# Gated attention and Fourier mixing on one core: the order of the projections' sums, fillers and maxima

## The chip, the cores and the metric

The kernel runs on one core of a Trainium2 chip. A core has five engines with queues of their own: TensorE (PE; PEld is its weight load), VectorE (DVE), ScalarE (ACT), GpSimd (POOL) and SyncE (SP), which here issues the DMA transfers. Engines run at once and wait for one another by semaphores; within a queue the order is fixed. The metric is the device time of one execution in microseconds (us). The time before is the median of three runs.

## The reference

Only what is computed; x is [2048, 640] and S = 2048, D = 640, 32 heads of 20.

```python
def reference(A_x, A_wqkv, A_wo, B_x, B_dft_seq_re, B_dft_seq_im, B_dft_hid_re, B_dft_hid_im, gate_w):
    def _A_ref(x, wqkv, wo):
        ...
        q, k, v = qkv[0], qkv[1], qkv[2]
        scores = jnp.einsum("bhqd,bhkd->bhqk", q, k) * (Dh ** -0.5)
        p = _softmax(scores, axis=-1)
        o = jnp.einsum("bhqk,bhkd->bhqd", p, v)
        return (lambda x, *d: x.transpose(*d))(o, 0, 2, 1, 3).reshape(B, S, D) @ wo
    def _B_ref(x, dft_seq_re, dft_seq_im, dft_hid_re, dft_hid_im):
        a = jnp.einsum("bsd,ed->bse", x, dft_hid_re)
        b = jnp.einsum("bsd,ed->bse", x, dft_hid_im)
        y = jnp.einsum("ts,bse->bte", dft_seq_re, a) - jnp.einsum("ts,bse->bte", dft_seq_im, b)
        return y
    x = A_x
    g = _sigmoid((x * gate_w).sum(-1, keepdims=True))
    a = _A_ref(x, A_wqkv, A_wo)
    b = _B_ref(x, B_dft_seq_re, B_dft_seq_im, B_dft_hid_re, B_dft_hid_im)
    return g * a + (1 - g) * b
```

## The kernel before

All products are made from float32 values cut in two parts of fewer bits ("split": ACT or POOL casts the high part, DVE or POOL subtracts to get the low one), three matmuls for one product (`three`, L118 to L120).

The program has a prologue and a long steady part. The prologue, about 276 us, makes q, k and v; the steady part walks 32 units of attention (scores, exponentials, p times v) with the Fourier products between them as filler. The change is in the prologue alone. Its pieces:

- **x** is four blocks of 512 rows, `xs[0]` to `xs[3]`, each loaded as raw float32 into `pair_tile`s (pool "p", seven of them) and split (`load_x`, `load_first`).
- **q and k tiles**: five column tiles c of 128 for q and five for k. Tile 0 is projected plainly for each block (`qk_tiles`, 30 matmuls). Tiles 1 to 4 are projected by **quads** (`quad`): for a **group** g of two blocks, x block 2g and 2g+1, a quad makes q and k of column c in seven products instead of eight, p6, p7, p1, p5, p2, p4, p3 in that order, 54 matmuls with 512 columns. It needs sums of x over its two blocks (s1 to s5, `load_sums`, made on POOL and split by ACT and DVE) and sums of weights (`load_pair`, which gives three steps: `sums` on POOL, L403 to L407; `ready`, the first set of parts, "t"; `parts`, the second set, "b", one of its two casts by POOL in the second group). PE's products go to PSUM banks, of which six rotate; ACT and DVE add them up (L444), POOL adds one output (L459) and cuts the outputs in parts (L115), and SP stores them to `qk_scr`. Between its products a quad calls `between(k)`, where the next quad's steps are hung in.
- **Value pairs** (`v_pair(hf, s)`, 30 matmuls): v of half the heads for two tiles of 128 rows. POOL fills the tile with ones, ACT copies the products into it, SP stores it.
- **Maxima**: the attention needs row maxima of the scores before its exponentials. `run_s` issues steps of two score matmuls each (L196); DVE reduces each bank (L198). 41 steps (82 maxima) are done ahead in the prologue. They read the first **stack** of q and k rows, twelve loads from `qk_scr` (`load_stack`).
- **Segments** (`lead`): eight tiles of the hidden-dimension Fourier product are made in the prologue, fifteen pieces of two matmuls each (L511), with maxima between the pieces; they need `wb` weights 2, loaded by `load_wb(2)`.

The order is written out by hand in the program, line after line: an instruction's place in its engine's queue is where the code issues it. In the order before: blocks 0 and 1, value pairs, quads of the first group, blocks 2 and 3, value pairs with maxima, quads of the second group with two segments each. SP's queue takes every load and store in that order as well, and an issue waits for a free semaphore lane and for what its transfer reads.

## Time and profile before

| | |
|---|---|
| time, three runs | 1861.7, 1864.7, 1865.28 us; median 1864.7 |
| the profiled execution | 1868.31 us, its span 1866.5 us |
| mean granted TensorE clock | 0.993 |
| busy | PE 1841.1 us (99%), DVE 1448.6 (78%), ACT 1392.5 (75%), POOL 1057.8 (57%) |
| HBM | 224.97 MB read, 64.05 MB written |

In the profile a row of a timeline is: start in us, duration, engine, line, operation, out<-in, shapes, count, and in brackets the engine's idle time before it and what ended that. A busy time of a stretch counts overlapping matmuls once, and matmul ends are modelled, so PE can read as busy while it goes slowly; the distance from one matmul's start to the next says more. Releasers are inferred from semaphores. The span lies within the execution's own time.

### The profile page before, as it was taken

To read this page: it belongs to the slowest core of one execution; us is meant where nothing else is said; L and a number is where in the kernel's file an instruction comes from. 1 tells how busy PE (TensorE), PEld (TensorE's weight loads), DVE (VectorE), ACT (ScalarE), POOL (GpSimd) and SP (SyncE) were. 2 spreads that over 40 slices of the span, in tenths; PEclk is the share of its full clock that TensorE was granted. 3 is DMA by queue.
4 is the path that set the end of the run, shared out by engine and by line. 5 is a ranking of instruction groups with operands and counts; after the bars stand their busy time and mean duration, and the time that the engine had idled before them with its cause. 6 is when DMAs were issued, how large, how long until landed. Compare 5 with 4: busy or idle time off the path is not lost.

```text
span 1866.5 us, 44873 instructions
## 1 busy us (share of the span) xinstructions
PE 1841.1 (99%) x17520; PEld 1359.7 (73%) x17520; DVE 1448.6 (78%) x2426; ACT 1392.5 (75%) x2716; POOL 1057.8 (57%) x859
## 2 busy tenths in 40 slices
PE   9998999999999999999999999999999999999998
PEld 8787776776767777777777777777777777776666
DVE  4535777878878888888888888888888888888853
ACT  4543337878878888888888888888878877778885
POOL 4654663212126677344578778655668867745544
PEclk9998999999999999999999999999999999999999
DMA  7576334121226576545567586746586776531333
GB/s 251 180 244 166 111 131 123 46 78 58 75 61 170 177 224 194 149 125 143 179 192 237 166 242 200 199 148 168 175 230 192 209 206 194 178 94 49 88 99 108
DMA packets 185467, 291.95 MB, mean 156 GB/s; under 512 B 48211, under 2 KB 116435, under 8 KB 185255
## 3 DMA queue, kind: packets, MB, share of 16 engines
q1 hardware_dynamic: 185255, 289.09, 51.9%
q8 instruction: 137, 2.24, 0.5%
q14 instruction: 75, 0.61, 0.1%
HBM read 224.97 MB, written 64.05 MB: 155 GB/s over the span
## 4 chain that ended last, share of the span: by engine, by line
PE 90%; DMA 2%; issue 2%; POOL 2%; DVE 2%; ACT 1%; SPq 0%; POOLq 0%; DVEq 0%; ACTq 0%
PE ps L749 25%; PE yp L828 19%; PE ps L1144 17%; PE ps L196 14%; PE yp L511 7%; PE yp L935 3%; PE ps L118 2%; PE ps L120 2%; PE ps L119 2%; DVE part L115 1%; DVE mx L198 1%; DMA v_scr<-v 0%; DMA qst<-qk_scr 0%; DMA raw<-in_xa 0%; DVE p L444 0%
## 5 line engine op out<-in xcount | busy, mean ns | idle before, releaser
L198 DVE TENSOR_REDUCE mx<-ps 128x1 f32<-128x512 f32 x2048 | 1279.4, 683 | 255.8 <-PE ps L196 183.8
L1146 ACT ACTIVATE p<-ps 128x512 f32<-128x512 f32 x2048 | 1053.7, 613 | 282.4 <-PE ps L196 151.1
L1144 PE MATMUL ps<-qst,kst 62*128 62x512 f32 x1920 | 726.1, 406 | 0.1
L196 PE MATMUL ps<-kst,qst 60*128 60x512 f32 x1920 | 674.6, 412 | 13.9 <-DMA qst<-qk_scr 5.8
L828 PE MATMUL yp<-x,part 64*128 64x320 f32 x5376 | 628.7, 306 | 0.0
L828 PEld LDWEIGHTS yp<-x,part 64*128 64x128 f32 x5376 | 602.2, 185 | 5.7
L115 POOL TENSOR_TENSOR part<-raw,part 128x1024 fp32r<-128x1024 f32 (+3 forms) x136 | 299.4, 2203 | 339.9 <-ACT part L112 329.1
L749 PE MATMUL ps<-p,v 128*21 128x512 f32 (+1 forms) x4096 | 479.2, 595 | 0.0
L1144 PEld LDWEIGHTS ps<-qst,kst 62*128 62x128 f32 x1920 | 341.3, 185 | 162.7 <-DVE mx L198 97.4
L196 PEld LDWEIGHTS ps<-kst,qst 60*128 60x128 f32 x1920 | 326.4, 185 | 30.4 <-DVE mx L198 7.1
L749 PEld LDWEIGHTS ps<-p,v 128*21 128x21 f32 (+1 forms) x4096 | 103.9, 101 | 244.3 <-issue 237.2
L511 PE MATMUL yp<-wb,x 64*128 64x320 f32 x1920 | 229.9, 310 | 0.4 <-ACT raw L521 0.4
L511 PEld LDWEIGHTS yp<-wb,x 64*128 64x128 f32 x1920 | 212.5, 188 | 6.9 <-ACT raw L521 0.8
L708 POOL TENSOR_TENSOR raw<-raw,raw 128x1024 f32<-128x1024 f32 x77 | 187.5, 2436 | 0.0
L522 POOL TENSOR_TENSOR raw<-raw 128x320 f32<-128x320 f32 x56 | 48.6, 867 | 228.0 <-ACT raw L521 190.9
L112 ACT ACTIVATE part<-raw 128x1024 fp32r<-128x1024 f32 (+3 forms) x157 | 138.5, 898 | 8.3 <-POOL raw L407 4.0
L935 PE MATMUL yp<-x,part 64*128 64x320 f32 x768 | 102.2, 308 | 0.0
L115 POOL TENSOR_TENSOR x<-araw,x 128x320 fp32r<-128x320 f32 x112 | 97.5, 877 | 1.3
L935 PEld LDWEIGHTS yp<-x,part 64*128 64x128 f32 x768 | 91.9, 186 | 1.0
L731 POOL TENSOR_TENSOR araw<-araw 128x320 f32<-128x320 f32 x80 | 70.1, 887 | 0.2 <-DMA araw<-a_scr 0.2
L115 POOL TENSOR_TENSOR p<-p 128x512 fp32r<-128x512 f32 x40 | 54.6, 1379 | 25.6 <-ACT p L112 25.1
L962 POOL TENSOR_TENSOR yt<-yt,m 128x320 f32<-128x320 f32 x64 | 55.9, 886 | 2.3 <-DVE m L848 2.3
(126 smaller groups left out, 1484.5 us busy)
## 6 DMA issues: line engine op xcount, KB each, us to landing
raw<-in_cdft SPq DMA_DIRECT2D x192, 512.0 KB
araw<-a_scr SPq DMA_DIRECT2D x192, 160.0 KB
qk_scr<-p SPq DMA_DIRECT2D x40, 512.0 KB
kst<-qk_scr SPq DMA_DIRECT2D x90, 160.0 KB
qst<-qk_scr SPq DMA_DIRECT2D x90, 160.0 KB
yt<-y_scr SPq DMA_DIRECT2D x80, 160.0 KB
y_scr<-yt SPq DMA_DIRECT2D x64, 160.0 KB
a_scr<-raw SPq DMA_DIRECT2D x56, 160.0 KB
```

The costliest lines, as they stand in the source:

```text
L112: act.activation(dst1, src, AF.Copy)
L115: e2.tensor_tensor(dst2, src, f32(dst1), op=ALU.subtract)
L196: pe.matmul(ps, q[b : b + KROWS, qt * P : (qt + 1) * P], k[b : b + KROWS, kc * 512 : (kc + 1) * 512], start=True, stop=True)
L198: return lambda: dve.tensor_reduce(mx[n][:, h, qt, kc : kc + 1], ps, axis=AX.X, op=ALU.max)
L511: pe.matmul(yp[h][:, :HE], x[r, xz, d, cs], w[r, wz, d, :HE], start=d == 0 and z == 0, stop=d == ND - 1 and z == 2)
L708: pool.tensor_tensor(raws[0], raws[0], raws[1], op=ALU.add if PRODUCTS[n][0][1][0] > 0 else ALU.subtract)
L731: pool.tensor_tensor(raws[0], raws[0], raws[1], op=ALU.add if PRODUCTS[n][1][1][0] > 0 else ALU.subtract)
L749: pe.matmul(t[32 * j : 32 * j + m, :], v[:, r : r + m], pp[qc][:, h, :], start=kt == 0, stop=kt == NS - 1)
L828: pe.matmul(yp[h][:, :HE], c[r, cz, cs], a[r, az], start=s == 0 and z == 0, stop=s == NS - 1 and z == 2)
L935: pe.matmul(yp[h][:, :HE], o[oz][r], wos[d, hf][r, wz], start=d == 0 and z == 0, stop=end)
L1144: pe.matmul(pt, k[b : b + KROWS + 2, kt * P : (kt + 1) * P], q[b : b + KROWS + 2, qc * 512 : (qc + 1) * 512], start=True, stop=True)
L1146: act.activation(pts[n, kt, qc][:, h], pt, AF.Exp, scale=float(DH) ** -0.5)
```

## The change

1. `load_sums` no longer loads x again: it makes s1 to s5 from the raw tiles that `load_x` and `load_first` keep (`xr`), in place, by another order of additions. Ten loads fall away, five for each group. Because the raw tiles of x stay taken, `qk_tiles` puts its outputs in `raw_tile`s (four of them).
2. In `quads`, the weight sums of the next quad are issued at `between(0)` (after p6), its first set of parts at `between(1)` and its second at `between(3)`; before, it was 1, 2 and 3. A table of hooks, by quad and place, says what else is hung in, and there is a new place 4 at a quad's end.
3. Two value pairs, (1, 4) and (1, 6), move from before the first group's quads to between them and the q and k tiles of block 2. In the second half all four pairs (0, 8) to (0, 14) come after both tiles, with three of the stack's loads behind each instead of six behind each of two. `load_wb(2)` and the pair's weights are loaded behind these, and more `flush()` calls issue stores at once.
4. The maxima: three segments go behind value pairs (1, 10) to (1, 14). In the second group's quads there is one segment at `between(1)`, and four maxima or a second segment at `between(4)` (`between(3)` in the last quad).
5. `v_pair` fills only the elements that stay one (32 of 672 in each partition).

The diff, with some unchanged lines left out:

```diff
--- before.py
+++ after.py
@@ -268,17 +268,17 @@
...
 
+    xr = {}
+
     def load_x(t):
-        raws = []
-        for d in range(0, ND, 2):
-            n = min(2, ND - d)
-            raw = pair_tile()[:, :n]
-            sp.dma_start(raw, xa[t, :, d : d + n])
-            raws.append((d, n, raw))
+        xr[t] = [pair_tile()[:, : min(2, ND - d)] for d in range(0, ND, 2)]
+        for k, raw in enumerate(xr[t]):
+            sp.dma_start(raw, xa[t, :, 2 * k : 2 * k + raw.shape[1]])
 
         def finish():
-            for d, n, raw in raws:
-                split(xs[t][:, 0, d : d + n], xs[t][:, 1, d : d + n], raw, act, dve)
+            for k, raw in enumerate(xr[t]):
+                d = slice(2 * k, 2 * k + raw.shape[1])
+                split(xs[t][:, 0, d], xs[t][:, 1, d], raw, act, dve)
 
...
@@ -304,10 +304,12 @@
...
             wt[k * ND] = [[parts[d][:, z, k] for d in range(ND)] for z in range(2)]
+        xr[0] = []
         for d in range(ND):
...
                 x = pair_tile()
+                xr[0].append(x[:, : min(2, ND - d)])
             sp.dma_start(x[:, d % 2], xa[0, :, d])
...
@@ -352,39 +354,44 @@
...
         for c, ps in zip(cs, pss):
-            st = pair_tile()
+            st = raw_tile().rearrange("p (z c) -> p z c", z=2)
             act.activation(st[:, 1], ps, AF.Copy)
...
     def load_sums(g):
-        a = {}
-        for i, k in ((1, 0), (1, 1), (0, 0), (0, 1)):
-            a[i, k] = pair_tile()
-            sp.dma_start(a[i, k], xa[2 * g + i, :, 2 * k : 2 * k + 2])
-        b = pair_tile()
-        sp.dma_start(b, xa[2 * g : 2 * g + 2, :, ND - 1].rearrange("t p c -> p t c"))
+        a, b = xr[2 * g], xr[2 * g + 1]
         if g:
...
         ops[g] = [t.rearrange("p (z d c) -> p z d c", z=2, c=512) for t in homes]
-        yield
         s1, s2, s3, s4, s5 = ops[g]
-        sums = (
-            (s1, a[1, 1], a[1, 0], a[1, 1], ALU.add),
-            (s3, a[1, 0], a[0, 0], a[1, 0], ALU.subtract),
-            (s2, a[0, 0], a[1, 1], a[0, 0], ALU.subtract),
-            (s4, a[0, 1], a[0, 1], a[0, 0], ALU.subtract),
-            (s5, b[:, :1], b[:, :1], b[:, 1:], ALU.subtract),
-        )
-        for t, u, u1, u2, op in sums:
-            pool.tensor_tensor(u, u1, u2, op=op)
-            yield
+
+        def add(out_, x, y, op=ALU.subtract):
+            pool.tensor_tensor(out_, x, y, op=op)
+
+        def cast(t, u):
             split(t[:, 0], t[:, 1], u, act, dve)
-            yield
+
+        return iter((
+            lambda: add(b[1], b[0], b[1], ALU.add),
+            lambda: add(b[0], a[0], b[0]),
+            lambda: add(a[0], b[1], a[0]),
+            lambda: cast(s2, a[0]),
+            lambda: cast(s3, b[0]),
+            lambda: cast(s1, b[1]),
+            lambda: add(a[1], a[1], a[0]),
+            lambda: cast(s4, a[1]),
+            lambda: add(a[2], a[2], b[2]),
+            lambda: cast(s5, a[2]),
+        ))
+
+    def go(stages, n=1):
+        for fn in itertools.islice(stages, n):
+            fn()
 
...
@@ -470,6 +477,7 @@
...
         done(o12, 0, 1)
+        between(4)
 
...
@@ -479,8 +487,9 @@
...
     def v_pair(hf, s):
-        vst = v_tile().rearrange("p (a k e) -> p a k e", a=NP // 2, k=2)
-        pool.memset(vst, 1.0)
+        vst = v_tile()
+        pool.memset(vst.rearrange("p (i e) -> p i e", e=DH + 1)[:, :, DH], 1.0)
+        vst = vst.rearrange("p (a k e) -> p a k e", a=NP // 2, k=2)
         for k in range(2):
...
@@ -555,31 +564,28 @@
...
     fin = load_wb(1)
+    flush()
     qk_tiles((0, ND), 1)
     sums = load_sums(0)
-    next(sums)
-    v_pair(0, 0)
     fin()
     soon = [load_pair(1)]
+    v_pair(0, 0)
+    go(sums)
+    flush()
+    soon.append(load_pair(2))
     v_pair(0, 2)
-    next(sums)
+    go(sums, 2)
     v_pair(0, 4)
-    next(sums), next(sums)
+    go(sums)
+    soon[0][1]()
     v_pair(0, 6)
-    next(sums), next(sums)
+    go(sums)
+    soon[0][2]()
     v_pair(1, 0)
-    next(sums), next(sums)
-    soon[0][1]()
+    go(sums, 2)
+    soon[0][3]()
     v_pair(1, 2)
-    next(sums), next(sums)
-    soon[0][2]()
-    soon.append(load_pair(2))
-    fin = load_x(2)
-    v_pair(1, 4)
-    next(sums)
-    soon[0][3]()
-    v_pair(1, 6)
-    fin()
+    go(sums, 2)
     flush()
...
@@ -595,74 +601,97 @@
...
 
-    def quads(g, soon, rest):
+    def quads(g, soon, hooks):
         for c in range(1, ND):
-            this = soon[c - 1]
             after = soon[c] if c + 1 < ND else None
...
             def between(k):
-                if k == 0:
-                    if c + 2 < ND:
-                        soon.append(load_pair(c + 2, pool if g else dve))
-                    elif c + 2 == ND:
-                        soon.extend(rest[0]())
-                elif k == 1 and g:
-                    lead(0, 5, 8, 2)
-                if k and after:
-                    after[k]()
-                elif k in (1, 2):
-                    rest[k]()
-                if g and k == 2 and c == 1:
-                    run_s(step + 2)
-                if g and k == 2 and c == ND - 1:
-                    load_v(0)
-
-            if g:
-                lead(0, 5, 6, 4, 0) if c == ND - 1 else lead(0, 5, 8, 2)
-            quad(c, g, this, between)
-
-    fins = []
-    quads(0, soon, (lambda: fins.extend(load_wqk(k) for k in (0, ND)) or [], lambda: fins.pop(0)(), lambda: fins.pop(0)()))
+                if k == 0 and c + 2 < ND:
+                    soon.append(load_pair(c + 2, pool if g else dve))
+                if k == 0 and after:
+                    after[1]()
+                hooks.get((c, k), lambda: None)()
+                if k in (1, 3) and after:
+                    after[2 if k == 1 else 3]()
+
+            quad(c, g, soon[c - 1], between)
+
+    fins = {}
+
+    def later_fin(key, load, *args):
+        def run():
+            fins[key] = load(*args)
+
+        return run
+
+    def finish(key):
+        return lambda: fins[key]()
+
+    def both(*fns):
+        return lambda: [fn() for fn in fns]
+
+    quads(0, soon, {
+        (1, 1): lambda: go(sums),
+        (3, 0): both(later_fin("k", load_wqk, 0), later_fin("q", load_wqk, ND)),
+        (4, 1): finish("k"),
+        (4, 2): later_fin("x", load_x, 2),
+        (4, 3): finish("q"),
+    })
+    flush()
     fin = load_x(3)
     pool.memset(f32(kst[0]), 1.0)
+    v_pair(1, 4)
+    fins["x"]()
+    v_pair(1, 6)
+    fin()
     qk_tiles((0, ND), 2)
-    v_pair(0, 8)
-    fin()
     sums = load_sums(1)
-    next(sums)
-    v_pair(0, 10)
+    go(sums)
+    flush()
     qk_tiles((0, ND), 3)
...
     stack = list(load_stack(0))
-    for s in (12, 14):
+    for s in range(8, NS, 2):
         v_pair(0, s)
         flush()
-        for args in stack[3 * s - 36 : 3 * s - 30]:
+        for args in stack[3 * (s // 2 - 4) : 3 * (s // 2 - 3)]:
             sp.dma_start(*args)
-        next(sums)
-        if s == 14:
-            next(sums)
+        go(sums, 2)
+    go(sums)
+    fin = load_wb(2)
     soon = [load_pair(1, pool)]
...
         v_pair(1, s)
+        flush()
         if s == 8:
-            flush()
-            fin = load_wb(2)
+            run_s(step + 2)
+            fin()
+            soon[0][1]()
         else:
-            run_s(step + 2)
-        if s < 14:
-            next(sums), next(sums)
+            lead(0, 5, 8, 2)
         if s == 10:
-            fin()
+            soon[0][2]()
         if s == 12:
-            soon[0][1]()
-            soon[0][2]()
+            soon[0][3]()
             soon.append(load_pair(2, pool))
-        if s == 14:
-            next(sums)
-            soon[0][3]()
     make_gate()
-    quads(1, soon, (lambda: fins.append(load_wb(3, act, pool)) or [], lambda: fins.pop()(), lambda: None))
+    four = functools.partial(lead, 0, 5, 8, 2)
+
+    def two():
+        run_s(step + 2)
+
+    quads(1, soon, {
+        (3, 0): later_fin("b", load_wb, 3, act, pool),
+        (4, 2): functools.partial(load_v, 0),
+        (1, 1): four,
+        (1, 4): two,
+        (2, 1): four,
+        (2, 4): two,
+        (3, 1): four,
+        (3, 4): four,
+        (4, 1): both(functools.partial(lead, 0, 5, 6, 4, 0), finish("b")),
+        (4, 3): two,
+    })
     pool.memset(f32(kst[1]), 1.0)
...
```

Three places in the built program's instruction order. POOL, first group, around the output add of a quad; before (the rows of L403 to L407 are the next quad's weight sums, the four L115 the output splits):

```order
L459 TENSOR_TENSOR p<-p 128x512
L403 TENSOR_TENSOR raw<-raw 128x256
L404 TENSOR_TENSOR raw<-raw 128x256
L405 TENSOR_TENSOR raw<-raw 128x256
L407 TENSOR_TENSOR raw<-raw 128x128 x2
L115 TENSOR_TENSOR p<-p 128x512 x4
```

and in the change, where L410 to L414 are the same sums and L466 the same add:

```order
L410 TENSOR_TENSOR raw<-raw 128x256
L411 TENSOR_TENSOR raw<-raw 128x256
L412 TENSOR_TENSOR raw<-raw 128x256
L414 TENSOR_TENSOR raw<-raw 128x128 x2
L466 TENSOR_TENSOR p<-p 128x512
L115 TENSOR_TENSOR p<-p 128x512 x4
```

The sums moved ahead of the add, behind the four splits of the quad before.

SP, around the first stack's loads (kst and qst), before:

```order
L346 DMA qk_scr<-p 128x2x512 x2
L346 DMA v_scr<-v 128x8x84
L641 DMA kst_87<-qk_scr 20x4x512 x6
L346 DMA v_scr<-v 128x8x84
L641 DMA qst_89<-qk_scr 20x4x512 x6
L397 DMA raw<-in_wqk 128x640 x2
L346 DMA v_scr<-v 128x8x84
L331 DMA raw<-in_wb 128x966
```

and in the change:

```order
L348 DMA qk_scr<-raw 128x2x512 x4
L348 DMA v_scr<-v 128x8x84
L658 DMA kst_87<-qk_scr 20x4x512 x3
L348 DMA v_scr<-v 128x8x84
L658 DMA kst_87<-qk_scr 20x4x512 x3
L348 DMA v_scr<-v 128x8x84
L658 DMA qst_89<-qk_scr 20x4x512 x3
L348 DMA v_scr<-v 128x8x84
L658 DMA qst_89<-qk_scr 20x4x512 x3
L333 DMA raw<-in_wb 128x966
```

The twelve loads are spread over four value pairs, each with its store ahead, and the `wb` load comes right behind them.

DVE, second group, quad 1, from the add of p2 (L444, in the change L451; the L115 rows are the first set of parts, L198 the maxima), before:

```order
L444 TENSOR_TENSOR p<-p,ps_1742 128x512
L115 TENSOR_TENSOR part<-raw,part 128x256
L115 TENSOR_TENSOR part<-raw,part 128x384 x2
L198 TENSOR_REDUCE mx<-ps_1763 128x1
L198 TENSOR_REDUCE mx<-ps_1765 128x1
L198 TENSOR_REDUCE mx<-ps_1769 128x1
L198 TENSOR_REDUCE mx<-ps_1771 128x1
L444 TENSOR_TENSOR p<-p,ps_1775 128x512
L444 TENSOR_TENSOR p<-p,ps_1794 128x512
```

and in the change:

```order
L115 TENSOR_TENSOR part<-raw,part 128x256
L115 TENSOR_TENSOR part<-raw,part 128x384 x2
L451 TENSOR_TENSOR p<-p,ps_1827 128x512
L451 TENSOR_TENSOR p<-p,ps_1841 128x512
L451 TENSOR_TENSOR p<-p,ps_1860 128x512
L198 TENSOR_REDUCE mx<-ps_1874 128x1
L198 TENSOR_REDUCE mx<-ps_1876 128x1
L198 TENSOR_REDUCE mx<-ps_1880 128x1
L198 TENSOR_REDUCE mx<-ps_1882 128x1
```

The parts stand ahead of the add of p2, and the four maxima behind all of the quad's adds.

## The prediction

> **What bounds the kernel now.** I read four views in this order: the page, the busy time by stretches, the waits of PE, and PE's timeline where those waits lie. From the page, the engines' busy time:
>
> ```profile
> PE 1841.1 (99%) x17520; PEld 1359.7 (73%) x17520; DVE 1448.6 (78%) x2426; ACT 1392.5 (75%) x2716; POOL 1057.8 (57%) x859
> ```
>
> PE bounds the program. Busy time by stretches (per engine busy us and instructions, then clock, DMA share, GB/s):
>
> ```profile
> 56.20:112.80 56.60, 52.13 (x216) 40.89 (x215) 35.43 (x49) 29.01 (x58) 35.27 (x34) 0.97 0.50 167
> 112.80:153.70 40.90, 40.90 (x244) 38.29 (x242) 9.63 (x8) 14.68 (x27) 19.80 (x17) 1.00 0.89 266
> 153.70:168.70 15.00, 9.18 (x36) 7.67 (x34) 6.15 (x7) 3.97 (x9) 8.03 (x7) 0.66 0.78 196
> 400.00:450.00 50.00, 50.00 (x503) 35.21 (x502) 40.38 (x70) 39.99 (x83) 13.34 (x13) 1.00 0.20 62
> ```
>
> From about 300 us on PE never stops, and the change leaves that part's instructions in their order. What can move is the prologue. PE's longest waits there, 56 to 276 us (total, times, longest):
>
> ```profile
> PE ps L196 <- DMA qst<-qk_scr: 5.8, 2, 3.1
> PE ps L196 <- DVE p L444: 3.7, 2, 2.6
> PE ps L196 <- DVE mx L198: 2.9, 2, 1.7
> ```
>
> These 12.4 us, all before maxima, understate the loss: waits for parts come on top, and a stall also costs the clock and slows the matmuls after it. So I count work against time. PE's timeline at the places used below:
>
> ```profile
> 68.66 0.39 PE L119 MATMUL ps<-x,part 128*128 128x512 f32 x1
> 68.89 0.40 PE L120 MATMUL ps<-x,part 128*128 128x512 f32 x1
> 71.46 0.80 PE L118 MATMUL ps<-kst,part 128*128 128x512 f32 x1 [2.17 <-ACT part L112]
> ...
> 153.51 0.31 PE L119 MATMUL ps<-wb,x 128*128 128x322 f32 x1
> 153.66 0.30 PE L120 MATMUL ps<-wb,x 128*128 128x322 f32 x1
> 157.05 0.76 PE L196 MATMUL ps<-kst,qst 60*128 60x512 f32 x1 [3.09 <-DMA qst<-qk_scr]
> 160.54 1.19 PE L196 MATMUL ps<-kst,qst 60*128 60x512 f32 x3 [2.73 <-DMA qst<-qk_scr]
> 161.66 0.64 PE L118 MATMUL ps<-wb,x 128*128 128x322 f32 x1
> ...
> 214.84 0.73 PE L196 MATMUL ps<-kst,qst 60*128 60x512 f32 x4
> 215.40 0.90 PE L511 MATMUL yp<-wb,x 64*128 64x320 f32 x10
> ...
> 218.46 0.50 PE L118 MATMUL ps<-x,part 128*128 128x512 f32 x1
> ```
>
> Unhindered starts lie 0.23 us apart for a 512-wide matmul (68.66, 68.89) and 0.15 for a value matmul (153.51, 153.66). Four maxima take 0.56 (214.84 to 215.40), and a segment of eight maxima with fifteen hidden pieces 3.62 (214.84 to 218.46). The groups of PE between 153.7 and 271.5 give the amounts:
>
> ```profile
> L511 PE MATMUL yp<-wb,x 64*128 64x320 f32 x240 | 28.1, 331 | 0.0
> L196 PE MATMUL ps<-kst,qst 60*128 60x512 f32 x82 | 25.9, 479 | 13.3 <-DMA qst<-qk_scr 5.8 <-DVE p L444 3.7 <-DVE mx L198 2.9
> ```
>
> A, quads of the first group (56.2 to 112.8): 216 matmuls x 0.23 = 49.7 of 56.6 us, so 6.9 lost. B, the first maxima: from 153.81 to 161.66 four maxima take 7.85 instead of 0.56, 7.3 lost; then matmuls at half clock to 167.0 (second row below) lose half of 5.3, 2.7. Together 10.0. C, from there to 271.5, where the steady part begins: the whole stretch from 153.81 is 117.7 us and holds 60 value matmuls (9.0), 216 quad matmuls as in the first group (49.7), eight segments (240 pieces; 29.2 with the last one's two extra maxima) and four fours (2.2), 90.1. That is 27.6 lost, 17.6 beside B. **A + B + C = 34.5 us** is what the change can reach.
>
> **The change part by part.** *Weight sums a group ahead (A, and most of C).* Quad 1 of the first group on POOL and DVE:
>
> ```profile
> 67.48 1.30 POOL L459 TENSOR_TENSOR p<-p 128x512 f32<-128x512 f32 x1 [6.83 <-DMA raw<-in_wqk]
> 68.74 0.74 POOL L403 TENSOR_TENSOR raw<-raw 128x256 f32<-128x256 f32 x1
> 71.04 1.14 POOL L407 TENSOR_TENSOR raw<-raw 128x128 f32<-128x128 f32 x2
> 75.92 1.28 DVE L115 TENSOR_TENSOR part<-raw,part 128x640 fp32r<-128x640 f32 x2
> ```
>
> POOL stands 6.83 us idle, then adds outputs (L459), and only then makes the next quad's weight sums (68.74 to 72.18, 3.4 us); ACT and DVE cut them into parts behind that, and PE, at 68.89, needs them. The change issues the sums after the first product, into that idle time. A quad is 54 x 0.23 = 12.4 us. POOL's last split for the quad before ends about 2.8 us into it (1.3 us each, four in a row), the sums end near 6, the output add waits for the fourth product at 6.2 anyway, ACT casts near 7 to 8.5 and DVE follows by 9. They are wanted at 12.4, and the second set (two DVE splits of 1.28 in all, after the sixth product at 10.4) at 15.2. Both have 3 us to spare. The weight loads are issued a whole quad before. A leaves 0.4 for its first quad; gain **6.5**.
>
> In the second group the same late sums block DVE's queue: maxima stand behind splits that wait for POOL, and PE waits for the banks that the maxima free:
>
> ```profile
> 198.62 2.63 DVE L115 TENSOR_TENSOR part<-raw,part 128x384 fp32r<-128x384 f32 x2 [0.91 <-ACT part L112]
> 201.17 2.47 DVE L198 TENSOR_REDUCE mx<-ps 128x1 f32<-128x512 f32 x4
> 203.56 0.67 DVE L444 TENSOR_TENSOR p<-p,ps 128x512 f32<-128x512 f32 x1
> ```
>
> *Maxima in smaller places* takes the pressure off too. Before, two segments fall on each quad: sixteen maxima x 0.60 (2.47 less one, by three) in bursts of eight. Now a quad has one segment and one four: PE 12.4 + 3.6 + 0.6 = 16.6 us, DVE 12 x 0.6 + 6 x 0.67 + about 3 for splits = 14.2. The third set of segments goes between value pairs, where DVE has 8.0 us (4.4 + 3.6) for 4.8 of maxima. What is left: in quads 2 and 3 the second set's low part is made on POOL behind the output splits, done about 0.7 us before PE wants it, or late if DVE is slowed, 0.7 each; the fourth quad has fourteen maxima with ten in a burst, 1.0; three segments between value pairs 0.5 each. That leaves 3.9, gain **13.7**.
>
> [...] If every first set of splits in the second group took some 1.5 us more, C would gain 4 us less: that is the second rival.
>
> *Filler and the stack loads (B).* SP, the chain of waits, and ACT (start, us):
>
> ```profile
> 142.41 2.30 SPq L641 DMA_DIRECT2D kst<-qk_scr  x6
> 146.08 5.73 SPq L641 DMA_DIRECT2D qst<-qk_scr  x6
> 139.46 2.89 DMA qk_scr<-p
> 151.46 8.84 DMA qst<-qk_scr
> 164.40 1.64 ACT L112 ACTIVATE wb<-raw 128x966 fp32r<-128x966 f32 x2 [8.27 <-DMA raw<-in_wb]
> ```
>
> Twelve loads issued from 142.41 on have landed by 160.5, 1.5 us each with the stores among them, and the last takes 8.84 from issue. In the change the order is three loads after each of four value pairs, so 3 x 1.5 = 4.5 us of transfer every 4.4 us: they just keep up. The last three are issued some 1.5 us after the fourth pair's end, one value pair (4.4 us) before the second maximum needs them: 2.9 us ahead. In these 1.5 us is the wait that the added flushes bring: SP stands until the pair's store can go, with the loads behind it. If they take 2.9, as the store at 139.46, nothing is lost; at 8.84 it is 6.0 and a half-clock window. I take 4.9, one backlog of three loads, so 2.0 lost, and a half-clock window:
>
> ```profile
> 71.50:74.80 3.30, 3.30 (x8) 2.62 (x9) 2.40 (x3) 1.98 (x4) 3.30 (x3) 0.50 0.14 52
> 156.90:167.00 10.10, 7.22 (x24) 6.16 (x25) 5.26 (x7) 2.14 (x4) 3.54 (x3) 0.50 0.74 199
> ```
>
> A stop of 2.17 us at 68.89 was followed by 3.3 us at half clock, so 1.7 more. B leaves 3.7 (0 to 7.7); gain **6.3**. [...] The weights of the hidden tiles are issued right behind these loads, and PE now wants them one value pair after the first maxima, not two. With 8.84 us like the loads, ACT's casts (1.64 at 164.40) and DVE's behind them they are ready some 11.5 us after issue; PE, which gets there 7.6 us after it unheld (2.2 to the first maximum, then 0.5 + 4.4 + 0.5) and 11.3 held as above, comes at about the same time. I cost them at nothing.
>
> *Sums from x's own loads.* Ten loads of 512 KB go (two sets of five). They cost PE nothing before (112.8 to 153.7: 40.90 of 40.90 busy), so nothing is gained directly. What they covered changes: x's raw tiles stay held, the outputs of the first projections move to the four raw tiles, and loads of weights for value columns and for pair 1 wait for those. ACT may stand several us for a store there; PE has six banks and needs the first of the waiting ones 8 us later. Cost 0, if that cover went at most 2. POOL's work up to the first quad is short enough:
>
> ```profile
> 45.30 0.66 POOL L483 MEMSET v<- 128x672 f32 x1
> 45.92 2.79 POOL L384 TENSOR_TENSOR p<-p 128x1024 f32<-128x1024 f32 x1
> ```
>
> Three adds of 2.8 and one set of sums (3.4) must stand before the quads, 11.8 us from about 26, with the quads at 56.2 - 8.9 = 47.3 since two pairs moved. *The fill of ones* writes 32 elements 84 bytes apart instead of 672; no row shows that form. Between 0.1 and 0.66, I take 0.3; POOL is not on PE's path there.
>
> **Sum.** 6.5 + 13.7 + 6.3 = 26.5 us. The profiled execution took 1868.31 us (span 1866.5, 1.8 outside), 3.6 above the median; so 1841.8 for such a run and **1838 us** against the median of 1864.7. With A, B and C fully regained it is 1830; with B at 7.7 and C at half, 1847.
>
> **The rivals.** *The first maxima still wait.* For it: the loads just keep up, and weights are issued behind them. Against: the 512 KB loads that filled the queue before them are gone. At 8.84 us from issue B gains 2.3 instead of 6.3, and the hidden weights may stop PE 3 us more: 1845.
> *POOL and DVE collide.* For it: the rows at 198.62 and 75.92, and POOL's chain in the second group with 0.7 us to spare. Against: DVE has 2.4 us free per quad. C then gains 9.7, not 13.7: 1842.
> *The sums come no earlier*, because a raw tile or a load holds them. Then A and C stay, and B's 6.3 with 2 of C remain: 1856. Against it: POOL's idle 6.83 us before L459.
> *Slower: the strided fill.* If a strided fill cost m us, POOL's sums for the first quads (three fills ahead of them, 8 us of room) would come 3m - 8 late, and the last stack loads (four fills ahead of the stores before them, 7 us of room) 4m - 7. Below 1.8 us all of it hides; at 6 it costs 10 + 17 us and the gain is gone; at 8 it costs 41 and the time is 1879. For it: no row shows the form. Against it: a plain fill of 672 elements takes 0.66.
>
> **How the numbers follow.** My forecast (1832 to 1841) has 0.62, the first rival 0.14, the second 0.13, no earlier sums 0.06, the slower one 0.05. The range 1830 to 1849 holds the first three, 0.86 at most and rather 0.8. About 0.2%, 3.7 us, is what a measurement can tell: faster 0.92, same 0.03 (half of the case without earlier sums, should it lose its 2 us of C and more), slower 0.05.
>
> **What would show it.** In the first group's quads PE's stretch should be near 50 us with no wait on a part above 0.5; DVE's maxima should follow each other with no split of 384 waiting for POOL between them; PE's wait for qst should be one of about 2 us with one half-clock window. The forecast is wrong if PE waits for `wb` at the first hidden piece, if waits on L198's banks remain above 6 us in sum, or if any wait shows before the quads.

## The result, and the profile after

The changed kernel takes 1847.6 us (median of 1845.92 to 1848.57; four runs), the kernel before 1864.4: a ratio of 0.9911, interval 0.9894 to 0.9929. That is 16.8 us faster where 26.5 were forecast; the time lies in the stated range and near the first rival's 1845, above the forecast's own 1832 to 1841. The profiled execution took 1848.57 us, its span 1846.8. One execution of run 2 below (1980.49 us at a granted clock of 0.85) is left out of its median, and one of the kernel before (1886.61 us at 0.943) draws the ratios of runs 1 to 4 to 0.001 to 0.003 below those of the medians and widens their intervals, so for these the medians say more. From its page, the engines' busy time:

```profile
PE 1829.8 (99%) x17520; PEld 1353.1 (73%) x17520; DVE 1451.8 (79%) x2426; ACT 1391.3 (75%) x2716; POOL 1049.4 (57%) x859
```

The prologue by stages, in the view of busy time by stretches (per engine busy us and instructions, clock, DMA share, GB/s): the last two value pairs and the first 18 quad matmuls, the rest of the first group's quads, the first maxima with the value pair behind them, and all from there to the steady part.

```profile
38.17:58.76 20.59, 16.25 (x80) 13.73 (x79) 11.56 (x9) 9.52 (x22) 13.41 (x16) 0.83 0.59 142
58.76:104.97 46.21, 45.94 (x200) 37.11 (x198) 33.58 (x42) 22.93 (x44) 30.36 (x28) 1.00 0.58 199
149.85:162.43 12.58, 7.47 (x37) 6.34 (x36) 4.94 (x6) 2.64 (x6) 3.34 (x5) 0.73 0.68 174
162.43:253.57 91.14, 90.94 (x594) 74.69 (x594) 71.78 (x120) 32.71 (x73) 53.33 (x57) 1.00 0.40 131
```

Counted as in the prediction (matmuls times their unhindered distance, 0.148 and 0.2305 us where the prediction has 0.15 and 0.23; in the change's trace starts lie 0.148 us apart from 127.88 to 149.62 and 0.230 from 58.54 to 79.96), the second row loses 46.21 - 198 x 0.2305 = 0.6: A is regained. The fourth loses some 1.9 with the last quad's end: C is regained but for that. The third holds four maxima and 30 value matmuls, 5.0 of 12.58 us: B still loses 7.6. And the first holds 60 value and 18 quad matmuls, 13.0 of 20.59: **7.6 us are lost at a place where only 0.5 was lost before**; I call it D. PE's timeline at the two places:

```profile
47.30 0.30 PE L120 MATMUL ps<-wb,x 128*128 128x322 f32 x1
49.30 0.50 PE L118 MATMUL ps<-kst,part 128*128 128x512 f32 x1 [1.70 <-ACT part L112]
49.64 0.39 PE L119 MATMUL ps<-kst,part 128*128 128x512 f32 x1
52.23 0.79 PE L120 MATMUL ps<-kst,part 128*128 128x512 f32 x1 [2.20 <-DVE part L115]
...
149.85 0.50 PE L196 MATMUL ps<-kst,qst 60*128 60x512 f32 x1
155.46 1.19 PE L196 MATMUL ps<-kst,qst 60*128 60x512 f32 x3 [5.11 <-DMA qst<-qk_scr]
156.58 0.63 PE L118 MATMUL ps<-wb,x 128*128 128x322 f32 x1
```

D is a wait for the first quad's parts, on ACT and then on DVE, and the half clock behind it (granted 0.50 from 50.08 to 56.90, with starts 0.43 us apart from 52.82 on). The reason stands in the queues of SP, ACT and POOL:

```profile
30.31 3.29 SPq L404 DMA_DIRECT2D raw<-in_wqk  x2
33.65 0.94 SPq L348 DMA_DIRECT2D qk_scr<-raw  x2
34.69 1.15 SPq L348 DMA_DIRECT2D v_scr<-v  x1
...
29.27 1.40 ACT L496 ACTIVATE v<-ps 128x320 f32<-128x320 f32 x4
42.40 0.77 ACT L496 ACTIVATE v<-ps 128x320 f32<-128x320 f32 x2 [11.72 <-DMA v_scr<-v]
47.23 0.77 ACT L496 ACTIVATE v<-ps 128x320 f32<-128x320 f32 x2 [3.12 <-DMA v_scr<-v]
48.83 1.24 ACT L112 ACTIVATE part<-raw 128x256 fp32r<-128x256 f32 x3
...
42.40 0.16 POOL L491 MEMSET v<- 128x32 f32 x1 [4.44 <-DMA v_scr<-v]
42.60 0.73 POOL L410 TENSOR_TENSOR raw<-raw 128x256 f32<-128x256 f32 x1
```

There are two value tiles. The third pair's fill and copies need the first pair's store to have landed, at 42.40, and the fourth pair's copies the second's, at 47.23. Behind them in their queues stand POOL's weight sums (42.60) and ACT's casts (48.83) for the first quad. The stores were issued late, at 34.69 and 39.88: SP stood at the weight loads of pair 1, at the first until 30.31 and 2.5 us more at the second, because DVE still read their raw tiles (a split of `wb`), and the stores stand behind these loads and those of pair 2. In the kernel before the outputs of block 1's tiles were not in raw tiles, and the same stop ended at 39.67, with two more value pairs to come before the quads:

```profile
39.67 0.77 ACT L487 ACTIVATE v<-ps 128x320 f32<-128x320 f32 x2 [9.41 <-POOL v L483]
```

### The profile page after: what moved, and what is told of

Its sections match the earlier page's. It is cut to its first block, busy times and chain, and to the rows that moved or that the text cites. A ratio compares the mean times of both kernels' runs of the same rounds, so it can differ in the third digit from the quotient of the medians.

```text
span 1846.8 us, 44851 instructions
## 1 busy us (share of the span) xinstructions
PE 1829.8 (99%) x17520; PEld 1353.1 (73%) x17520; DVE 1451.8 (79%) x2426; ACT 1391.3 (75%) x2716; POOL 1049.4 (57%) x859
## 4 chain that ended last, share of the span: by engine, by line
PE 93%; DMA 2%; issue 1%; DVE 1%; POOL 1%; ACT 1%; SPq 0%; POOLq 0%; ACTq 0%; DVEq 0%
PE ps L778 25%; PE yp L857 20%; PE ps L1173 17%; PE ps L196 15%; PE yp L520 7%; PE yp L964 3%; PE ps L118 2%; PE ps L120 2%; PE ps L119 2%; DMA v_scr<-v 1%; DMA qk_scr<-raw 1%; DMA p<-in_xa 1%; DVE part L115 0%; DMA qst<-qk_scr 0%; POOL p L115 0%
## 5 line engine op out<-in xcount | busy, mean ns | idle before, releaser
L198 DVE TENSOR_REDUCE mx<-ps 128x1 f32<-128x512 f32 x2048 | 1280.1, 684 | 257.1 <-PE ps L196 201.2
L196 PE MATMUL ps<-kst,qst 60*128 60x512 f32 x1920 | 667.2, 410 | 5.3 <-DMA qst<-qk_scr 5.1
L115 POOL TENSOR_TENSOR part<-raw,part 128x1024 fp32r<-128x1024 f32 (+3 forms) x136 | 297.7, 2191 | 331.8 <-ACT part L112 304.3
L520 PE MATMUL yp<-wb,x 64*128 64x320 f32 x1920 | 224.1, 307 | 0.0
L115 POOL TENSOR_TENSOR x<-araw,x 128x320 fp32r<-128x320 f32 x112 | 97.4, 877 | 1.3
L115 POOL TENSOR_TENSOR p<-p 128x512 fp32r<-128x512 f32 x32 | 43.3, 1359 | 21.5 <-ACT p L112 21.1
```

Of the source, the lines that this page charges most:

```text
L115: e2.tensor_tensor(dst2, src, f32(dst1), op=ALU.subtract)
L196: pe.matmul(ps, q[b : b + KROWS, qt * P : (qt + 1) * P], k[b : b + KROWS, kc * 512 : (kc + 1) * 512], start=True, stop=True)
L198: return lambda: dve.tensor_reduce(mx[n][:, h, qt, kc : kc + 1], ps, axis=AX.X, op=ALU.max)
L520: pe.matmul(yp[h][:, :HE], x[r, xz, d, cs], w[r, wz, d, :HE], start=d == 0 and z == 0, stop=d == ND - 1 and z == 2)
```

## Experiments

Each kernel is the changed one with the edit shown. The table gives the median time, the ratio to the kernel before with its interval, and what the profiled execution lost at each place, counted as above in us (B with the value pair ahead of the maxima where their first wait falls there; "x" is waits for block 2's and 3's x).

| kernel | median | ratio | D | A | B | C | x |
|---|---|---|---|---|---|---|---|
| before | 1864.4 | 1 | 0.5 | 7.0 | 9.8 | 17.8 | 0 |
| change | 1847.6 | 0.9911 (0.9894 to 0.9929) | 7.6 | 0.6 | 7.6 | 1.9 | 0 |
| 1 value stores first | 1841.8 | 0.9861 (0.9802 to 0.9920) | 0.0 | 0.6 | 5.5 | 1.9 | 0 |
| 2 pair (1, 4) back | 1844.2 | 0.9871 (0.9801 to 0.9942) | 1.9 | 0.6 | 7.1 | 1.9 | 0.7 |
| 3 x loaded again | 1846.7 | 0.9888 (0.9818 to 0.9958) | 2.4 | 0.5 | 11.3 | 1.9 | 0 |
| 4 late sums | 1858.9 | 0.9966 (0.9940 to 0.9992) | 6.9 | 3.9 | 7.5 | 11.1 | 0 |
| 5 stack loads earlier | 1847.2 | 0.9915 (0.9898 to 0.9932) | 6.0 | 0.6 | 7.2 | 1.9 | 0 |
| 6 hidden weights later | 1845.4 | 0.9901 (0.9887 to 0.9916) | 6.1 | 0.6 | 3.1 | 1.9 | 0 |
| 7 maxima in bursts | 1849.1 | 0.9922 (0.9907 to 0.9937) | 6.5 | 0.6 | 5.3 | 2.5 | 0 |
| 8 = 1 and 5 | 1841.2 | 0.9879 (0.9864 to 0.9894) | 0.6 | 0.7 | 7.2 | 1.9 | 0 |
| 9 = 1, loads early, hidden weights ahead | 1840.1 | 0.9873 (0.9858 to 0.9888) | 0.0 | 0.6 | 5.8 | 1.9 | 0 |
| 10 = 9, six loads first | 1840.2 | 0.9871 (0.9856 to 0.9886) | 0.6 | 0.7 | 5.3 | 1.9 | 0 |
| 11 full fill | 1851.0 | 0.9927 (0.9911 to 0.9944) | 7.1 | 0.5 | 8.2 | 3.4 | 0.6 |
| 12 = 9, pair (1, 6) later | 1839.7 | 0.9862 (0.9843 to 0.9880) | 0.2 | 0.7 | 4.3 | 1.9 | 1.6 |

**1, value stores first.**

```diff
-    soon = [load_pair(1)]
     v_pair(0, 0)
     go(sums)
     flush()
-    soon.append(load_pair(2))
     v_pair(0, 2)
+    flush()
+    soon = [load_pair(1)]
+    soon.append(load_pair(2))
     go(sums, 2)
```

> The change with one difference: the value stores of pairs (0, 0) and (0, 2) are issued before the weight loads of pairs 1 and 2, not behind them. Theory 1 (SP's queue): in the changed kernel SP stands until 33.24 us at a weight load whose raw tile DVE still reads, and the value store behind it lands at 42.40, where ACT and POOL go on; so here the store is issued near 31, ACT's long stop ends by 36 instead of 42.4, PE enters the first quads at 47.3 without a wait, the 7.6 us lost between 47.3 and 58.8 fall below 1.5, and the time is about 1841, 6 to 7 us under the change. Theory 2 (lost cover): the stop is an old one (it ended at 39.67 before the change too) and what hurts is that two value pairs no longer stand between it and the quads; then an earlier store helps by no more than the 3.4 us by which the change had made the stop later, and some 4 us of the 7.6 stay.

Its SP and ACT queues, and PE at the first quad:

```profile
30.48 2.95 SPq L348 DMA_DIRECT2D v_scr<-v  x2
33.52 2.23 SPq L404 DMA_DIRECT2D raw<-in_wqk  x4
...
34.79 0.77 ACT L496 ACTIVATE v<-ps 128x320 f32<-128x320 f32 x2 [3.73 <-DMA v_scr<-v]
...
47.46 0.31 PE L120 MATMUL ps<-wb,x 128*128 128x322 f32 x1
47.60 0.40 PE L118 MATMUL ps<-kst,part 128*128 128x512 f32 x1
```

The store goes out at 30.48 and has landed by 34.79; PE passes into the quads without a wait. D is 0.0 instead of 7.6 and the time falls by 5.8 us. Theory 1 holds; theory 2, by which some 4 us would stay, is out.

**2, pair (1, 4) back** ahead of the first group's quads, its place behind them left empty.

```diff
     v_pair(1, 2)
     go(sums, 2)
+    v_pair(1, 4)
     flush()
...
-    v_pair(1, 4)
     fins["x"]()
     v_pair(1, 6)
```

> The change with value pair (1, 4) put back ahead of the first group's quads (4.4 us of PE work as cover); (1, 6) stays behind them. Both theories on the wait before the quads expect it to shrink by the 4.4 us of cover: the waits of 2.0 and 2.58 us and the half clock go, the 7.6 us lost there fall to about 1. If POOL and DVE were simply too slow for the adds, splits and weight sums there, the loss would shrink too, but the splits would keep their 2.9 us and a wait for DVE would stay. On the other side the filler after the quads is one pair shorter, and block 2's x (loads issued at 100.3, cast from 110.0) may be waited for: 0 to 3 us. Time 1841 to 1844.

4.4 us of cover take 5.6 of the 7.6 us away; one wait of 1.6 us for DVE's split is left, which the expectation had as the sign of slow splits (see the rivals below), and 0.7 is paid for block 2's x. So cover would have done too, for less: the store's late issue is the cause, and the missing pairs are why it shows.

**3, x loaded again.**

```diff
-        a, b = xr[2 * g], xr[2 * g + 1]
+        a = {}
+        for i, k in ((1, 0), (1, 1), (0, 0), (0, 1)):
+            a[i, k] = pair_tile()
+            sp.dma_start(a[i, k], xa[2 * g + i, :, 2 * k : 2 * k + 2])
...
-            st = raw_tile().rearrange("p (z c) -> p z c", z=2)
+            st = pair_tile()
```

> The change with its first part undone: x loaded again for its sums (ten loads of 512 KB) and the outputs of the q and k tiles back in pair tiles, everything else as changed. Theory 1 (SP's queue) says that the raw tiles are then free, the weight loads no longer hold SP, and the value stores go out near 27.5 as before the change; with 2.6 MB of x ahead of them they land near 39 instead of 42.4, and the next pair's stop ends near 42 instead of 47.2. The 7.6 us lost at the first quads fall to 2 or less, the second group stays as changed, time about 1842. If the first part of the change has nothing to do with it (POOL's adds or the missing cover alone), the 7.6 us stay and the time is 1847 or, with the DMA queue fuller again before the stack's loads, 1850.

Its waits of PE from 20 to 252 us:

```profile
PE ps L196 <- DMA qst<-qk_scr: 8.5, 2, 5.6
PE ps L120 <- DVE part L115: 2.2, 2, 2.1
```

and ACT at the first stop and at the q and k tiles of block 3:

```profile
38.10 0.77 ACT L501 ACTIVATE v<-ps 128x320 f32<-128x320 f32 x2 [8.23 <-DMA v_scr<-v]
...
124.86 0.60 ACT L358 ACTIVATE p<-ps 128x512 f32<-128x512 f32 x1 [7.56 <-DMA qk_scr<-p]
```

Half as expected: the first stop ends at 38.10 instead of 42.40 and D falls to 2.4, so the raw tiles taken by the first part of the change are what made the store late. But B grows from 7.6 to 11.3, more than the 9.8 of the kernel before, and the time is the change's within a microsecond. The stack's loads take as long as in the change, 21.5 us from the first issue to the release of PE (132.00 to 153.46), but they start 12.5 us before PE is through with the work ahead of the maxima, not 15.9. The outputs of block 3's tiles, which they read, came late: ACT waited 7.56 us until an earlier store had freed the pair tile that it writes. The prediction has "nothing is gained directly" from the ten loads; together with the outputs' move to raw tiles they are worth 3.7 us at B in the changed order, more than the 2.3 that B gained in all. As far as one execution of each tells (the landings varied by 2 us, below), the filler pairs and the spread loads alone gained nothing at B.

**4, late sums.**

```diff
-                if k == 0 and after:
-                    after[1]()
                 hooks.get((c, k), lambda: None)()
-                if k in (1, 3) and after:
-                    after[2 if k == 1 else 3]()
+                if k in (1, 2, 3) and after:
+                    after[k]()
```

> The change with its second part undone: weight sums and both sets of parts hung in at places 1, 2 and 3 of a quad again, not 0, 1 and 3. If the late sums caused the losses A and most of C, the first group's quads take 6 us more than their 50 (1.4 us waits for parts, as at 68.89, 89.12 and 102.8 before the change), and the second group 4 to 10 us more, because maxima stand behind splits that wait for POOL: time 1858 to 1864. If the smaller places of the maxima alone carry C, the second group changes by less than 2 us and the time is about 1854.

DVE in the second group's first quad, first of the change, then of this kernel:

```profile
189.49 4.87 DVE L198 TENSOR_REDUCE mx<-ps 128x1 f32<-128x512 f32 x8
194.28 2.45 DVE L115 TENSOR_TENSOR part<-raw,part 128x256 fp32r<-128x256 f32 x3
196.65 1.27 DVE L451 TENSOR_TENSOR p<-p,ps 128x512 f32<-128x512 f32 x2
```

```profile
196.55 0.67 DVE L451 TENSOR_TENSOR p<-p,ps 128x512 f32<-128x512 f32 x1
198.52 0.42 DVE L115 TENSOR_TENSOR part<-raw,part 128x256 fp32r<-128x256 f32 x1 [1.29 <-ACT part L112]
199.86 2.62 DVE L115 TENSOR_TENSOR part<-raw,part 128x384 fp32r<-128x384 f32 x2 [0.91 <-ACT part L112]
202.40 1.27 DVE L451 TENSOR_TENSOR p<-p,ps 128x512 f32<-128x512 f32 x2
```

The median rises by 11.3 us; in the traces A loses 3.3 more than in the change and C 9.2 (D 0.7 less). In the change the three splits run one after another without a wait; here DVE stands twice at them and PE's banks stay full behind (PE's three waits on L451, 5.2 us in sum). The expectation held for C. In A it was 6 and came as 3.3. The other 3 us of the kernel before lie at its first stop, 68.89 to 71.46: 2.57 us between starts and a stretch at half clock behind it (granted 0.50 from 71.47 to 74.88), where run 4 has 1.54 us between starts. There, before the change, ACT came late to the copies of the first quad's products (L448), behind the casts of x's sums and a value copy that a fill held up:

```profile
60.69 0.45 ACT L487 ACTIVATE v<-ps 128x320 f32<-128x320 f32 x1 [1.92 <-POOL v L483]
...
63.86 0.62 ACT L448 ACTIVATE p<-ps 128x512 f32<-128x512 f32 x1
```

That fill had waited 4.70 us, to 60.00, for a value store. So these 3 us look like the value tiles' stop once more and not like the place of the sums; this is read from the trace, no run tries it.

**7, maxima in bursts.**

```diff
-        else:
-            lead(0, 5, 8, 2)
+        elif s < 14:
+            run_s(step + 2)
...
+    four()
     quads(1, soon, {
...
-        (1, 4): two,
+        (1, 2): two,
+        (1, 4): four,
         (2, 1): four,
-        (2, 4): two,
+        (2, 4): four,
...
```

> The change with its fourth part undone: no segments behind value pairs, two segments in each of the second group's quads again (one ahead of it, one at place 1), four maxima at place 2 of the first, the weight sums as changed. If the early sums carry the gain of the second group, the bursts of eight maxima cost 2 to 4 us there: time 1850 to 1852. If the smaller places carry half of it, 8 us come back: 1855 or more. Three segments move behind the value pairs in the change; the waits for the stack's loads stay as they are.

C loses 2.5 instead of 1.9, less than the expected 2 to 4, and the median is 1.5 us higher, within the intervals. With the sums early the places of the maxima hardly matter. With the sums late they seem to: run 4 loses 11.1 in C, the kernel before 17.8, though these two differ in more than the places. The two parts cover the same stall, and the sums alone nearly suffice.

**5 and 8, stack loads one pair earlier** (8 with the edit of 1).

```diff
...
+    load_rows(3)
     for s in range(8, NS, 2):
         v_pair(0, s)
         flush()
-        for args in stack[3 * (s // 2 - 4) : 3 * (s // 2 - 3)]:
-            sp.dma_start(*args)
+        if s < 14:
+            load_rows(3)
+        if s == 12:
+            fin = load_wb(2)
+            soon = [load_pair(1, pool)]
...
-    fin = load_wb(2)
-    soon = [load_pair(1, pool)]
```

> The change with the first stack's loads one value pair earlier: three right behind the stores of the q and k tiles, three behind each of the next three value pairs, and the hidden weights and pair 1's weights one value pair earlier too. Theory 1 (the loads form a queue that starts too late): the last load lands some 4.4 us earlier, near 151 instead of 155.4, the wait of 5.61 us before the second maximum falls to about 1.2 and the half clock behind it goes; the hidden weights are cut by 156, when PE gets there near 157. Time 1847.6 - 5 to 6, about 1842. Theory 2 (the DMA engines are full: 12 loads, four value stores and the weights need their time whatever the order): the last landing comes less than 2 us earlier, the value stores later, and the time stays above 1845.

> The change with two differences: value stores ahead of the weight loads (as in the first run, which measured 1841.8) and the stack's loads and the hidden weights one value pair earlier. If the two losses are separate, the 5.7 us that the first run still lost at the first maxima (a wait of 3.68 and the half clock behind it) fall below 1.5 and the time is 1837 to 1838. If the DMA engines are full there, it stays at 1841.

In 5 the loads were issued earlier, the wait fell from 5.61 to 4.64 us between starts, and B from 7.6 to 7.2. In 8 the last load was issued at 137.61 and PE was released at 148.48, over 10 us later. Theory 2 holds in both times (1847.2 and 1841.2): the earlier issue did not bring the data earlier by as much.

**6, hidden weights later.** `load_wb(2)` and `load_pair(1, pool)` behind `v_pair(1, 8)`.

> The change with the loads of the hidden weights and of pair 1's weights one value pair later, behind the store of value pair (1, 8). If these loads share the DMA engines with the last three stack loads and slow them, the wait of 5.61 us for the stack falls by about 2; in exchange the weights, 8.2 us from issue to landing and 4 us of cutting, come near 164 and PE waits some 3 us for them at the first hidden piece: time 1847 to 1850. If the weights do not slow the stack's loads, the wait stays at 5.6 and the 3 us at the hidden piece (or none, if PE comes later) are all that changes: 1848 to 1851.

PE waited 2.82 us for the stack, no half clock followed (granted 1.00 from 146.81 to 157.05, below), and the weights were not late; B was 3.1. That is the expected direction but it shows nothing: up to the first maxima run 7 issues the same instructions as the change, and waited 3.48 there, the change 5.61. The landing varied by 2 us between these two, and of two stops of nearly one length (2.82 and 2.77 us) one had a half clock behind it and one had none (below).

**9, 10 and 12.** In 9 `load_wb(2)` stands ahead of block 3's tiles, where the DMA engines are nearly idle (0.05 busy from 120 to 124 us in the change, 0.34 from 118 to 130), and three stack loads ahead of the first value store; 10 puts six there; 12 moves pair (1, 6) from between the halves to behind (0, 14).

> The version with both fixes (1841.2), with the hidden weights' loads moved ahead of the q and k tiles of block 3, where the DMA engines are nearly idle, and pair 1's weights back behind the last value pair of the first half. Theory (from the run with the weights later, where the wait for the stack fell from 5.6 to 2.8 us): 1.4 MB of weights behind the last stack loads take turns with them in the DMA engines; with the weights out of the way the twelve loads and three value stores are done some 4 to 5 us sooner, the wait of 5.24 us before the second maximum falls under 1, and the half clock behind it goes: time 1835 to 1837. Rival: the stack's loads themselves, at some 1.05 us each with the value stores between them, are the limit; then 2 to 3 us of wait stay and the time is 1839.

> The same with six stack loads instead of three ahead of the first value store, three behind each of the first two value pairs. If the order of stores and loads matters little (the engines work off what is there), the last load lands another 1 us or so earlier and the time is as in the run before, 1835 to 1837; if the value stores, now behind six loads, hold up ACT for a value tile, a wait for a bank or for parts shows on PE before the first maxima.

> The version with the value stores first and the hidden weights ahead (1840.1), with value pair (1, 6) moved from between the halves to just before the first maxima; the stack's loads so start 4.4 us earlier relative to PE. Theory (the queue's throughput is the limit: twelve loads of some 1.0 us each and four value stores of 1.4 us take 17 to 18 us from the stores of block 3's tiles on, whatever stands behind them): the last load lands near 142.5, when PE gets to the maxima at 142.8; the wait of 4.0 us falls under 1, no half clock follows, 5 us are gained there; PE waits 0.7 us for block 2's x, as in the run with a pair moved ahead of the quads. Time about 1836. Rival (the value store of the pair that is moved comes into the same queue and the loads end as late as before): wait of 3 to 4 us, time 1840 to 1841.

Run 9 from the first stack load's issue to the wait's end, in the view by stretches:

```profile
127.20:146.80 19.60, 16.13 (x108) 15.62 (x107) 6.76 (x6) 9.15 (x17) 6.23 (x7) 1.00 0.89 198
```

The weights are out of the way and the loads still take 19.6 us, as against 21.5 in the change (133.94 to 155.46), with the DMA engines 89% busy in the mean (85% in the change). The expected 4 to 5 us did not come; the rival's 2 to 3 us of wait did, and one more (4.0). In 10 the stack's wait is 1.01 us between starts, in 12 there is none, and another takes its place; PE's longest wait and its reason in run 12:

```profile
146.75 0.45 ACT L496 ACTIVATE v<-ps 128x320 f32<-128x320 f32 x1 [4.72 <-DMA v_scr<-v]
...
144.18 0.74 PE L196 MATMUL ps<-kst,qst 60*128 60x512 f32 x4
147.30 0.41 PE L118 MATMUL ps<-wb,x 128*128 128x322 f32 x1 [2.38 <-ACT logit L500]
```

ACT cannot copy the value pairs because their two tiles wait for their stores, so PE lacks a bank. Stack loads and value stores all go out from SP's queue, and in these runs the one that went later was waited for: the stack in 9 (4.0 us), a value store in 12 (4.72 us of ACT). The three end within 0.5 us of one another and of run 8 within 1.6. Run 12 has the lowest median, 7.9 us below the change, most of it (5.8) from the edit of run 1; it can't be told from runs 9 and 10. Run 12's expected 1836 did not come, and what B still loses was not regained.

**11, full fill.** `pool.memset(vst, 1.0)`, all 672 elements.

> The change with its fifth part undone: POOL fills all 672 elements of a value tile (0.66 us) instead of 32. The changed trace shows the strided fill at 0.16 to 0.17 us, so 0.5 us of POOL more per value pair, up to 3 us before the first quads: the weight sums and parts there come later, the loss at the first quads grows by 0 to 2 us, nothing else moves; time 1847 to 1849. If the fill is off the path everywhere: no difference.

3.4 us more in the median, outside the expected 1847 to 1849, with intervals of the ratio that overlap the change's. D did not grow (7.1); the trace has 1.5 us more in C and 0.6 each at B and for x. So the full fill does not act at the first quads, as far as one execution tells; whether it costs anything elsewhere stays open. The strided fill takes 0.16 to 0.18 us in each of its 16 instances in the change, the plain one took 0.66.

## Why the prediction was right or wrong

**A** (0.4 left expected, 0.6 measured) was right in its number and half right in its reason. Run 4 shows that the place of the sums is worth 3.3 us of A and 9.2 of C; the other 3 us of A went, by the trace, with other parts of the change. And the margin was not "3 us to spare". POOL, DVE and PE around the end of the second quad of the change, which begins at 67.06:

```profile
72.26 1.30 POOL L115 TENSOR_TENSOR p<-p 128x512 fp32r<-128x512 f32 x1 [1.76 <-ACT p L112]
73.52 0.74 POOL L410 TENSOR_TENSOR raw<-raw 128x256 f32<-128x256 f32 x1
75.86 1.15 POOL L414 TENSOR_TENSOR raw<-raw 128x128 f32<-128x128 f32 x2
77.60 1.56 DVE L115 TENSOR_TENSOR part<-raw,part 128x384 fp32r<-128x384 f32 x2 [0.91 <-ACT part L112]
79.50 0.39 PE L118 MATMUL ps<-kst,part 128*128 128x512 f32 x1
```

POOL's four splits of the quad before do not follow in a row; they wait for ACT's casts and end 6.5 us into the quad, not 2.8. The sums end at 10.0, not near 6, and the first parts at 79.16, 0.34 us before PE uses them. That it held was in part luck.

The loss left in **C** was sized too high: 3.9 expected, 1.9 measured. The 0.7 in quads 2 and 3 and the 0.5 per segment between value pairs did not come, and the prediction credited part of it to the maxima's places, which run 7 prices at 0.6 once the sums are early.

**The step that failed is "Sums from x's own loads": "Cost 0, if that cover went at most 2."** It measured 7.6 (D). The step saw that weight loads would wait for raw tiles and ACT for a store, and asked only whether PE has banks enough; PE showed no wait for one there. It did not ask what else stands behind the waiting copies on ACT and the waiting fill on POOL, which are the parts of the first quad. It did place the quads at 47.3, where PE comes to them, and counted POOL's work up to there (11.8 us from about 26) as if it could run without a stop; but POOL's next fill waits for the value store, and did so in the kernel before: the stop at 39.67 could have been read. Run 1 removes the loss, run 3 shows that the raw tiles made most of it (5.2 of 7.6), and run 2 that one pair of cover hides 5.6 of it.

**B** was right in its mechanism and wrong in its size: 3.7 left expected, 7.6 measured. The 2.3 gained are the first rival's price for the loads alone; the 3 us that it added for a stop at the hidden weights did not come. The step is "they just keep up": three loads in 4.5 us, taken from twelve loads in 18 us with two value stores among them, while four value stores run beside them now. The last load was issued about 147.7 and released PE at 155.46, 7.8 us, where 4.9 was taken. In runs 5, 8 and 9 an earlier issue or another order made the stream end little sooner, and in 10 and 12 it only changed who waits; the DMA engines were 85 to 89% busy in it (the change and run 9), so nearly full. The hidden weights were rightly costed at nothing: no wait for them shows.

In sum the terms were 6.5 + 13.7 + 6.3 = 26.5; measured 6.4 + 15.9 + 2.3 - 7.1 = 17.5 in the traces (D was 0.5 before), 16.8 in the medians; the two profiled spans differ by 19.7, the 2 us more lying behind the prologue. That the time fell into the range and near 1845 was partly luck: D stood in no term, and C's 2.2 us beyond the forecast cover a part of it. (The chances of the three cases that the range is said to hold add up to 0.89, not 0.86.) One of the listed signs of a wrong forecast, a wait ahead of the quads, is what came.

The rival of sums that come no earlier fell: A and C were regained. DVE's splits took longer while POOL worked. The first quad's three splits of parts (128x256 and two of 128x384; a row shows the shape of its first), in the kernel before with POOL idle (55.30 to 60.00), in the change beside POOL's sums (51.91 to 54.31), and in run 3:

```profile
56.56 1.36 DVE L115 TENSOR_TENSOR part<-raw,part 128x256 fp32r<-128x256 f32 x3
```

```profile
51.76 2.97 DVE L115 TENSOR_TENSOR part<-raw,part 128x256 fp32r<-128x256 f32 x3
```

```profile
44.24 5.22 DVE L115 TENSOR_TENSOR part<-raw,part 128x256 fp32r<-128x256 f32 x3
```

The same splits take 1.36, 2.97 and 5.22 us. That POOL's work slows them is the author's reading of the first two rows. In the second group, where the rival had its price (some 1.5 us more a set and 4 us in all, estimated from the rows at 198.62 and 75.92), no run shows it: the three splits of the change take 2.45 us at 194.28, but with the sums early they are ahead of need. At the first quads it seems to have one: what is left of D in runs 2 and 3 (1.9 and 2.4) is a wait for DVE's splits. No run separates it. The strided fill at 0.17 us leaves nothing of the slower case.

## What to carry to other kernels

Where a step takes a buffer from another pool, follow the queue that waits for that buffer, and then every instruction behind each of those that wait, on each engine, up to what PE needs first; a bank count alone does not answer it. An old stop that costs nothing because of work between it and its reader has to be priced before that work is moved away. Loads that were waited for in the nearly full stream of transfers here (85 to 89% busy) gained little from an earlier issue (B 7.6 to 7.2 in run 5) or from another order (5.8 in run 9 against 5.5 in run 1), and in run 12, where no wait for them was left, PE stood 2.77 us behind a value store. More PE work between helped little in run 12 (B 4.3 instead of run 9's 5.8, and 1.6 paid for x); that fewer transfers in the stream would do more is argued, not shown.

## What the runs showed of the hardware

**Half-clock stretches of 3.41 us.** In the prologue of the kernel before the granted clock was 0.50 for 3.41 us from 71.47, for 10.24 from 156.80 and for 3.41 each from 180.69, 204.59 and 252.37; in that of the change for 6.83 each from 50.08 and from 152.48. In each of these two traces the starts lie whole multiples of 3.41 us apart. Two stops of nearly the same length were not followed alike; the stretches with the stop and the next, first of run 6 (2.82 us between starts), then of run 12 (2.77):

```profile
146.81:150.22 3.41, 2.22 (x14) 1.71 (x12) 1.32 (x3) 0.66 (x4) 0.00 (x0) 1.00 0.69 174
150.22:153.64 3.42, 2.29 (x14) 1.95 (x15) 1.78 (x3) 0.00 (x0) 0.00 (x0) 1.00 1.06 265
153.64:157.05 3.41, 3.41 (x25) 3.17 (x25) 1.85 (x3) 2.38 (x5) 0.00 (x0) 1.00 0.79 265
```

```profile
145.09:148.50 3.41, 1.20 (x8) 1.20 (x9) 2.11 (x4) 1.75 (x6) 0.16 (x1) 1.00 0.75 205
148.50:151.91 3.41, 3.41 (x15) 3.41 (x14) 2.44 (x2) 1.16 (x4) 2.41 (x3) 0.50 0.41 102
```

In run 6 the stop fell over the border at 150.22, PE was busy 65 and 67% of the two stretches, and the clock stayed at 1.00. In run 12 it fell into one, 35% busy; the next ran at 0.50 and cost 1.7 us (estimated as half of 3.41). That the place of the stop makes the difference is the author's reading of this pair. In the kernel before PE was busy 37, 17, 61, 70 and 47% of the stretch ahead of the five half-clock places above, in the change 49 and 38% of those ahead of its two, by the records. Stretches with 63 to 75% were followed by full clock five times in the kernel before (72% from 88.53 and from 102.19, 71% from 197.76, 63% from 225.07, 75% from 245.55), so the share alone does not tell it. Where half clock went on for another stretch, PE had been busy 22 and 90% in the kernel before (from 156.80 and 160.21), 37 and 13% in the change (from 50.08 and 152.48).

**A transfer's landing varied by 2 us between two runs.** With the same instructions ahead of it, the second maximum waited 5.61 us in the change and 3.48 in run 7:

```profile
152.98 1.18 PE L196 MATMUL ps<-kst,qst 60*128 60x512 f32 x3 [2.98 <-DMA qst<-qk_scr]
```

From the issue of the last stack load to this maximum it was 7.8 us in the change (147.70 to 155.46) and 5.6 in run 7 (147.36 to 152.98). Whether this differs between executions or between chips stays open.
